# Taps of one token block moved from TensorE to VectorE in a fused sequence-mixing and feed-forward kernel

## The chip, the cores and the metric

The kernel runs on one core of one Trainium2 chip. Five engines of that core work side by side, each through its own queue in order: TensorE (PE in the profile; its weight loads are PEld), VectorE (DVE), ScalarE (ACT), GpSimd (POOL) and SyncE (SP), which here only issues transfers. The metric is the device time of one launch in microseconds, the median of several runs. Lower is better.

## The reference

All tensors are bf16. `q`, `k`, `v` are 2048 tokens by 640 channels.

```
x       = layernorm(q)
k_shift = sum over t in 0..3 of k[token - t] * shift_k[:, t]     # four taps per channel
kv      = k_shift * v
y       = causal long convolution of kv with ssm_k (2048 taps)   # by FFT
h       = q + x * (y + kv * ssm_D)
out     = h + (silu(LN(h) @ w_gate) * (LN(h) @ w_up)) @ w_down   # 640 -> 1728 -> 640
```

The part that the change touches is `k_shift * v`, for the last quarter of the tokens.

## The kernel before

**Blocks.** The 2048 tokens are cut into 4 blocks of 512. Partition p of a block holds tokens 4p to 4p+3, so a tile of a block is 128 x (4 x 640). For block i the kernel makes `kv` (the taps), takes its transform (`xf`), multiplies it with the transforms of the filter blocks (`p0i`, `p1i` and so on: product of token block j and filter block i-j, all summed into the tile Y of block i), transforms back (`iv`), adds the residual and normalises, and runs the feed-forward part (`fg` and `fu` for gate and up, `dn` for down). A feed-forward block has two halves of 256 tokens; names such as `fg2.11` mean block 2, half 1, group 1.

**Order.** Every operation is first recorded as a named task with the memory it reads and writes (`_Graph.add`). The dictionary `PLAN` then gives, for each engine, a list of task numbers: that is the order of its queue. `arrange` and `emit` only add the waits that memory, PSUM and the order require. Task numbers count the tasks in the order of recording. The string `units` gives each PSUM tile one of four units of two banks; a TensorE task that opens a tile waits until the former tile of that unit has been read.

**The taps of block 3 before.** `kvload(3)` records a transposing transfer `kT3` of 528 tokens of k (channels on partitions) into `kT` and the load `v3` of v into `kvo` (tasks 652 and 653). `taps(3)` records three groups, for channel pieces 0, 2 and 4 (tasks 654 to 662): `tp3.*` on TensorE (70 steps, each as two matmuls of 64 rows with the diagonal tap weights, L731), `ke3.*` on ScalarE (copy from PSUM to `XT`, L455) and `kv3.*` on VectorE (product with v, written over `kvo`, L742).

**What follows.** `xf3.jc` (L619) multiplies row j of `kvo`, that is the tokens 4p+j, with a cosine or sine table; its results are copied out by `xf3e.*` to `XH1` and `OS`, and `xb3.*` (L634) combine them on VectorE. The spectra then go into `p33`, `yb3.0` to `yb3.5` (L651) turn the sum into four rows, `iv3.*` (L919) transform back. For block 2 the same tasks are `yb2.*` and `iv2.*`: `iv2.0` and `iv2.1` need `yb2.4`, `iv2.2` and `iv2.3` need `yb2.5`. An `iv` is followed by `ivN.e` (ScalarE), `g` (VectorE), `m` and `s` (ScalarE statistics), `v` (VectorE), `r` (GpSimd), `n` (VectorE) and `ht` (a transposing transfer into `hnT`); the `fg` and `fu` of a half need the two `ht` of that half.

**Accumulating transfers.** `addto` (L568) issues from GpSimd a transfer that adds one SBUF tile to another. Several sums of the kernel are made so already, with 640 KB each.

**The branch of the change.** It is in the code before, but no block uses it (`DT` and `DTA` are empty):

```
load("wst", wst[...], ... [[0, P], [1, 4 * D]] ...)             # the 640 x 4 weights, to every partition
load("kh%d" % i, kh[...], ... (N * i - 3) * D, [[4 * D, P], [1, 7 * D]])   # seven tokens per partition
g.add("wbr", "act", ... out=wbr[:], in_=wst[:].rearrange("p d u -> p u d") ...)
for j0 in (1, 0):
    kin = [[-D, 4], [2 * D, 2], [1, D]] from kh[:, 3 + j0]      # 4 taps x 2 tokens x 640
    win = wbr[:].unsqueeze(2).to_broadcast([P, 4, 2, D])
    a: tm = kin * win                       # VectorE, 128 x 5120
    b: tm[:, 0:2] += tm[:, 2:4]             # transfer from GpSimd where i is in DTA, else VectorE
    c: tm[:, 0] += tm[:, 1]                 # VectorE, 128 x 1280
    d: kvo[:, j0:4:2] = tm[:, 0] * kvo[:, j0:4:2]   # VectorE, 128 x 1280
```

`kh` lies over `C2` and `wst` and `tm` lie over `XH1`, which the products `p13` read; `wbr` lies over `kT`.

Of the kernel before, what the change touches and what calls it, by code (L numbers as in the profile page):

```python
# [50 lines left out]
class _Graph:  # L51
# [128 lines left out]
    def emit(self, block):  # L180
# [74 lines left out]

PLAN = {
    "pe":
        "20 22 26 29 24 25 28 32 35 31 34 27 30 33 68 65 62 41 39 72 70 46 56 48 52 50 58 54 44 86 88 78 80 139 84 137 76 74 82 "
        "96 102 90 92 104 94 100 204 98 301 298 159 168 304 155 177 186 212 153 151 311 313 141 147 143 149 309 145 307 317 237 "
        "319 315 236 321 241 202 218 242 220 210 216 214 208 206 247 261 256 246 266 251 257 267 262 365 356 271 383 278 374 "  # L260
        "279 283 287 291 422 421 486 483 489 431 496 498 426 492 502 427 504 494 436 500 506 432 441 451 446 442 447 463 464 "
        "660 654 657 456 452 468 555 546 472 573 564 476 665 663 669 667 671 673 677 675 592 593 597 602 598 603 607 617 613 "
        "612 622 618 623 627 634 647 726 717 635 639 744 643 735 754 753 763 759 758 764 768 778 795 773 774 779 784 788 783 "
        "796 799 805 802 808 "
        "",
    "act":
        "1 18 5 37 36 40 73 71 57 49 53 51 59 55 45 89 79 87 81 140 138 77 85 75 83 97 103 91 93 105 95 101 205 99 302 299 160 "
        "169 162 305 163 171 178 172 213 187 156 152 312 154 142 148 314 150 144 146 308 189 318 310 190 239 320 316 180 322 "
        "238 181 243 203 329 219 221 211 217 215 209 207 330 331 332 333 244 334 335 258 336 249 337 338 248 339 268 252 254 "
        "253 263 259 264 340 357 366 272 384 276 359 269 360 273 274 368 280 277 375 369 377 284 386 378 288 387 424 423 487 "  # L270
        "484 490 292 433 497 499 428 503 493 429 495 505 501 507 437 434 514 515 516 438 517 443 439 518 519 448 444 461 520 "
        "521 449 522 523 453 465 524 661 655 525 658 457 454 458 459 469 556 547 558 559 549 550 574 565 576 577 567 666 670 "
        "668 568 674 678 676 594 595 685 599 600 686 604 688 689 690 605 608 691 610 609 692 693 614 615 694 619 695 620 624 "
        "625 628 630 629 727 718 729 720 730 721 745 747 736 748 738 739 756 755 761 760 766 765 770 769 771 775 776 793 781 "
        "780 786 785 791 789 790 794 "
        "",
    "dve":
        "23 21 38 69 66 67 64 63 42 43 116 108 109 47 110 112 113 111 117 114 115 118 120 119 121 60 122 61 124 123 126 127 128 "
        "130 129 132 131 134 133 135 106 136 161 196 170 107 164 306 303 300 173 166 195 175 188 199 198 157 179 324 191 200 "
        "323 201 325 240 182 326 193 327 184 328 197 222 345 344 347 346 245 348 350 349 352 351 341 250 353 255 354 260 355 "  # L280
        "395 392 358 393 265 394 270 367 398 275 361 385 400 363 403 370 376 405 372 397 399 402 404 379 407 388 408 381 409 "
        "425 488 485 491 410 390 412 411 414 413 417 416 508 509 430 510 418 511 435 512 419 513 440 531 530 533 532 445 534 "
        "450 536 535 541 526 537 538 540 539 542 543 455 544 460 528 662 462 557 545 548 656 560 473 659 551 562 575 566 553 "
        "582 477 578 664 672 679 680 569 580 681 571 682 683 596 583 584 585 587 588 589 687 601 590 701 702 606 704 703 611 "
        "706 707 709 708 616 696 697 621 632 626 711 631 633 712 714 713 699 715 716 728 719 636 731 722 733 724 640 746 737 "
        "644 740 749 700 757 648 751 742 762 767 772 777 782 787 792 797 800 806 803 809 "
        "",
    "pool":
        "19 17 15 16 125 165 174 158 192 183 223 225 224 342 396 362 281 371 285 401 380 289 406 389 343 293 420 415 527 466 "
        "470 561 474 552 478 579 570 684 586 591 529 705 710 698 637 732 723 641 645 750 649 741 "  # L290
        "",
    "sp":
        "0 2 3 8 4 6 10 7 230 9 11 13 14 235 296 226 12 229 297 227 481 231 167 176 228 234 295 233 194 185 482 232 364 282 373 "
        "290 391 294 286 382 480 653 652 471 563 554 467 475 479 581 572 651 734 725 638 752 646 743 642 650 798 807 801 804 "
        "810 "
        "",
    "units":
        "0131203132312001201201213230032110213023012230313133033220021021122013200230230222110332013110130232003210332301202110"
        "01310112312301210312031012210230131023033303012010313012013"
        "",  # L300
    "fills": {
        "wb0": ["zmem", 3],
        "k0t4.0": ["zmem", 1],
    },
}
# [2 lines left out]
def bass_sequential_preLN__ssm_conv_h3__swiglu_ffn__prompt_kernel(  # L308
# [43 lines left out]
    PAIR = True  # L352
    BN = (0,)
    BNH = ()
    DT = ()
    DTA = ()
    HALF = (0, 1, 2, 3)
    R4K = ()
    R4X = (1,2,3)
# [19 lines left out]
    with ExitStack() as es:  # L379
# [66 lines left out]
        def load(name, dst, src, kb, engs="sp", **kw):  # L446
            return g.add(name, engs, lambda e, n: e.dma_start(dst, src), ("ld", kb), w=[dst], dma=True, **kw)
# [119 lines left out]
        def addto(name, dst, src):  # L567
            return g.add(name, "pool", lambda e, n: e.dma_start(dst, src, accum_op=ALU.add, max_dma_last_dim=4096), ("acc", 2 * int(np.prod(dst.shape))),  # L568
                         r=[dst, src], w=[dst], dma=True)
# [117 lines left out]
        def kvload(i):  # L687
            if i in DT:
                load("wst", wst[:].rearrange("p d u -> p (d u)"), bass.AP(A_shift_k.tensor, A_shift_k.offset, [[0, P], [1, 4 * D]]), 655360)
                load("kh%d" % i, kh[:].rearrange("p j d -> p (j d)"), bass.AP(K2.tensor, K2.offset + (N * i - 3) * D, [[4 * D, P], [1, 7 * D]]), 1146880)  # L690
                load("v%d" % i, kvo[:], tokens(V2, i), 655360)
                return
            tload("kT%d" % i, kT[:], K2[N * i - 16:N * (i + 1), :], N + 16, D)
            load("v%d" % i, kvo[:], tokens(V2, i), 655360)

        def taps(i):
            if i in DT:
                g.add("wbr", "act", lambda e, n: e.activation(out=wbr[:], in_=wst[:].rearrange("p d u -> p u d"), func=ACTF.Copy), ("ac", 4 * D), r=[wst[:]], w=[wbr[:]])
                for j0 in (1, 0):
# [6 lines left out]
                          r=[kh[:], wbr[:]], w=[tm[:]])  # L706
                    if i in DTA:
                        addto(nm + "b", tm[:, 0:2], tm[:, 2:4])
# [517 lines left out]
```

## Time and profile before

| what | value |
|---|---|
| median of 3 runs | 260.73 us (259.1 to 261.67) |
| profiled execution | 259.3 us; its span 257.3 us |
| PE busy | 249.3 us, 97% of the span |
| DVE busy | 200.0 us, 78% |
| ACT busy | 184.5 us, 72% |
| POOL busy | 58.5 us, 23% |
| granted clock | 1.0 throughout |

The span runs from the first to the last instruction. A share of busy time is a mean over the span; which engine sets the time is read from the stage in question. The timeline lists instructions in order of start, neighbours of one kind merged; the time of an instruction is longer than the distance to the next one on the same engine, because neighbours overlap a little. For instance VectorE products of 128 x 5120 take 2.82 us each, and two that follow each other start 2.74 us apart. Sums over a queue are made from such distances.

### The profile page before, as it was taken

The page shows a single profiled execution, that of the slowest core. Times are in us where ns is not written, and L with a number is a line of the kernel's source. Part 1 is how long each engine was busy: PE and PEld are TensorE (multiplying, and loading weights), DVE is VectorE, ACT ScalarE, POOL GpSimd, SP SyncE. Part 2 cuts the span into 40 slices and gives each one's busy share as a digit, 9 for nine tenths or more (in the row PEclk, how much of TensorE's full clock was granted, in tenths as well). Part 3 has the DMA queues.
Part 4 walks back from the last instruction along what each step waited for, and adds up shares of the span by engine and source line. Part 5 has one row for each costly group of instructions (what it writes and reads, how often), then busy time and mean ns, then how long its engine had stood idle before and what let it go on. Part 6 is the DMA issues. An engine that isn't in the chain of part 4 may idle for free.

```text
span 257.3 us, 5303 instructions
## 1 busy us (share of the span) xinstructions
PE 249.3 (97%) x2253; PEld 195.1 (76%) x2253; DVE 200.0 (78%) x256; ACT 184.5 (72%) x302; POOL 58.5 (23%) x56
## 2 busy tenths in 40 slices
PE   7999997999999999979999999999999999999995
PEld 4878773587888766868888866788886678888763
DVE  3689999999999998999999988999958524211242
ACT  2489999999996894577899789749981854516410
POOL 1001003082312052860030813333230314000000
PEclk9999999999999999999999999999999999999999
DMA  6998946788994058786946035497870152700011
GB/s 220 335 328 210 402 155 133 221 205 190 329 190 87 0 82 124 128 164 153 273 87 124 3 51 117 118 221 133 148 135 3 25 104 33 149 0 3 0 42 60
DMA packets 37620, 35.29 MB, mean 137 GB/s; under 512 B 21203, under 2 KB 32478, under 8 KB 37598
## 3 DMA queue, kind: packets, MB, share of 16 engines
q1 hardware_dynamic: 31792, 23.82, 33.2%
q0 software_dynamic: 5792, 11.14, 25.1%
q8 instruction: 17, 0.28, 0.5%
q14 instruction: 5, 0.04, 0.1%
q10 hardware_dynamic: 14, 0.01, 0.0%
HBM read 16.55 MB, written 2.62 MB: 75 GB/s over the span
## 4 chain that ended last, share of the span: by engine, by line
PE 62%; DVE 20%; ACT 11%; DMA 5%; issue 1%; SPq 0%; DVEq 0%
PE ps L1029 32%; PE ps L1115 16%; DVE tt L777 6%; PE ps L599 3%; DMA Y<-tt 3%; DVE Y L777 3%; PE ps L731 2%; ACT KO L455 2%; PE ps L919 2%; ACT C L455 2%; PE ps L581 2%; DVE C L777 2%; PE ps L992 2%; PE ps L619 2%; DMA k0n<-in_A_k_dram 1%; DVE gu L1050 1%
## 5 line engine op out<-in xcount | busy, mean ns | idle before, releaser
L1115 PE MATMUL ps<-Wd,gu 128*128 128x320 bf16 (+1 forms) x420 | 58.7, 300 | 0.0
L1115 PEld LDWEIGHTS ps<-Wd,gu 128*128 128x128 bf16 (+1 forms) x420 | 38.7, 97 | 18.4 <-issue 3.6
L777 DVE TENSOR_TENSOR tt<-XH,C 128x2560 bf16<-128x2560 bf16 (+1 forms) x31 | 47.8, 1571 | 1.5 <-DMA Y<-tt 0.9
L1050 DVE TENSOR_TENSOR gu<-gu,ub 128x1024 bf16<-128x1024 bf16 (+1 forms) x32 | 19.8, 620 | 26.2 <-ACT gu L1037 13.7
L1037 ACT ACTIVATE gu<-ps 128x1024 bf16<-128x1024 f32 (+1 forms) x32 | 29.4, 923 | 12.1 <-PE ps L1029 12.0
L1029 PE MATMUL ps<-hnT,GB 128*128 128x256 bf16 x280 | 34.0, 273 | 0.9 <-ACT XT L455 0.9
L1042 ACT ACTIVATE ub<-ps 128x1024 bf16<-128x1024 f32 x24 | 24.6, 1024 | 13.3 <-PE ps L1029 11.5
L1029 PE MATMUL ps<-hnT,UB 128*128 128x256 bf16 x280 | 33.8, 273 | 0.0
L1029 PEld LDWEIGHTS ps<-hnT,GB 128*128 128x128 bf16 x280 | 27.3, 98 | 4.3 <-ACT XT L455 1.0
L1029 PEld LDWEIGHTS ps<-hnT,UB 128*128 128x128 bf16 x280 | 27.3, 98 | 3.4 <-ACT KO L455 0.2
L1029 PE MATMUL ps<-hnT,GA 128*128 128x256 bf16 x240 | 28.8, 273 | 0.0
L1029 PE MATMUL ps<-hnT,UA 128*128 128x256 bf16 x240 | 28.5, 273 | 0.1
L837 POOL TENSOR_TENSOR mv<-mv,half 128x1 f32<-128x1 f32 x16 | 21.3, 1335 | 24.7 <-DVE mv L835 24.7
L1029 PEld LDWEIGHTS ps<-hnT,UA 128*128 128x128 bf16 x240 | 23.4, 98 | 3.4 <-ACT C L455 0.5
L1029 PEld LDWEIGHTS ps<-hnT,GA 128*128 128x128 bf16 x240 | 23.4, 98 | 3.2 <-DVE XH L458 0.3
L840 ACT ACTIVATE qo<-xh 128x640 bf16<-128x640 bf16 x28 | 21.0, 749 | 5.7 <-DMA xh<-in_A_q_dram 3.2
L581 PE MATMUL ps<-KT,tab 128*128 128x320 bf16 x128 | 19.6, 300 | 1.6 <-ACT K3r L455 0.7
L934 ACT ACTIVATE qo<-ps,one,st 128x640 bf16<-128x640 f32 x16 | 13.7, 886 | 9.8 <-PE ps L919 9.0
L568 POOL DMA_DIRECT2D xh<-RB x12 | 10.7, 888 | 34.7 <-DVE RB L1132 23.2
L581 PEld LDWEIGHTS ps<-KT,tab 128*128 128x128 bf16 x128 | 11.5, 98 | 8.2 <-ACT K3r L455 1.6
L837 POOL TENSOR_TENSOR st<-st,half 128x4 f32<-128x4 f32 x4 | 7.9, 1986 | 33.6 <-DVE st L832 21.8
L455 ACT ACTIVATE XH<-ps 128x640 bf16<-128x640 f32 x19 | 13.3, 736 | 1.5 <-PE ps L619 0.7
(112 smaller groups left out, 384.8 us busy)
## 6 DMA issues: line engine op xcount, KB each, us to landing
C<-US POOLq DMA_DIRECT2D x6, 640.0 KB, 5.9
kc<-in_A_ssm_k_dram SPq DMA_DIRECT2D x4, 640.0 KB, 10.6
xh<-in_A_q_dram SPq DMA_DIRECT2D x4, 640.0 KB, 5.5
out_dram<-xh SPq DMA_DIRECT2D x15, 160.0 KB, 2.0
kvo<-in_A_v_dram SPq DMA_DIRECT2D x3, 640.0 KB, 4.4
xh<-RB POOLq DMA_DIRECT2D x12, 160.0 KB, 3.0
Wd<-in_B_w_down_dram SPq DMA_DIRECT2D x1, 1280.0 KB, 7.8
C<-K3r POOLq DMA_DIRECT2D x2, 640.0 KB, 7.9
```

Source lines behind the costliest of these rows:

```text
L455: return e.activation(out=dst[1], in_=src(), func=ACTF.Copy, scale=scale)
L568: return g.add(name, "pool", lambda e, n: e.dma_start(dst, src, accum_op=ALU.add, max_dma_last_dim=4096), ("acc", 2 * int(np.prod(dst.shap ...
L581: last = e.matmul(pt.f(c, W), tab[:, f, cs, j], src[:, j, c * W:(c + 1) * W], start=(j == js[0]), stop=(j == js[1]))
L777: g.add(nm, "dve", lambda e, n_: e.tensor_tensor(out=d, in0=a, in1=b, op=op), ("sb", n * D), r=[a, b], w=[d])
L837: g.add(name + "r", "pool", lambda e, n: e.tensor_tensor(out=dst, in0=tmp, in1=hf, op=ALU.pow), ("pp", 4), r=[tmp, half[:]], w=[dst])
L840: g.add(name + "m", "act", lambda e, n: e.activation(out=junk, in_=x, func=ACTF.Identity, scale=-1.0 / D, accum_out=sm), ("aa", D, 0), r=[ ...
L934: g.add(nm + "e", "act", lambda e, n, pt=pt, q2=q2, s=s, j=j: e.activation(out=q2, in_=pt.f2(W), func=ACTF.Identity, scale=s[:, 3, j:j + 1 ...
L1029: last = e.matmul(pt.f(q // 2, 256, o=256 * (q % 2)), w[:, c, f0:f0 + P], hnT[:, c, cols], start=(c == 0), stop=(c == NC5 - 1))
L1037: g.add("sg%d.%d%d" % (i, h, gp), "act", lambda e, n, pa=pa, gv=gv, nf=nf: e.activation(out=gv, in_=pa.f(0, 256 * nf).rearrange("p (f x) - ...
L1042: g.add("su%d.%d%d" % (i, h, gp), "act", lambda e, n, pb=pb: e.activation(out=ub[:].rearrange("p b x -> p (b x)"), in_=pb.f(0, 1024), func ...
L1050: g.add("mu%d.%d%d" % (i, h, gp), "dve", lambda e, n, gv=gv, ubv=ubv: e.tensor_tensor(out=gv, in0=gv, in1=ubv, op=ALU.mult), ("sb", 256 * ...
L1115: last = e.matmul(pt.f(c, W), gu[k, fb, col(i, j)], Wd[k, fb, c * W:(c + 1) * W], start=st, stop=sp)
```

## The change

`DT` and `DTA` become `(3,)`: block 3 takes the branch above, with sum b as an accumulating transfer. Tasks 652 to 662 (eleven) become 652 to 663 (twelve): `wst`, `kh3`, `v3`, `wbr`, `tv3.1a` to `tv3.1d` (656 to 659, for the odd tokens of each four), `tv3.0a` to `tv3.0d` (660 to 663, for the even ones). All later numbers rise by one, so `xf3.10` is 663 before and 664 after. The three PSUM tiles of `tp3` go. With it comes a whole new `PLAN`: other orders on all engines, other units, and some copies on another engine (of those near block 3: `rs1.2`, `rs1.3`, `rs2.2`, `rs2.3`, `xf3e.10`, `xf3e.00`, `la3.0x` and two `gd` go from VectorE to ScalarE, `xf3e.01` and `kf2e.000` from ScalarE to VectorE). The first filler of TensorE is put ahead of `wb4`, which now comes before `wb0`.

```
     "pe":
...
-        "660 654 657 456 452 468 555 546 472 573 564 476 665 663 669 667 671 673 677 675 592 593 597 602 598 603 607 617 613 "
...
+        "464 456 468 472 555 546 476 564 573 664 666 670 668 676 674 672 678 593 592 598 597 603 602 607 617 613 618 612 622 "
...
     "dve":
...
-        "450 536 535 541 526 537 538 540 539 542 543 455 544 460 528 662 462 557 545 548 656 560 473 659 551 562 575 566 553 "
-        "582 477 578 664 672 679 680 569 580 681 571 682 683 596 583 584 585 587 588 589 687 601 590 701 702 606 704 703 611 "
...
+        "409 425 410 485 488 491 412 411 381 414 413 430 416 417 508 509 418 510 435 511 419 512 440 513 656 530 445 531 532 "
+        "533 450 534 455 540 536 535 526 538 537 460 539 541 658 542 543 659 544 528 660 548 557 545 582 551 560 583 553 585 "
+        "562 662 584 663 566 680 681 675 575 682 683 684 587 596 569 578 588 590 580 571 589 601 702 703 704 705 606 708 707 "
...
-        "wb0": ["zmem", 3],
+        "wb4": ["zmem", 3],
...
-    DT = ()
-    DTA = ()
+    DT = (3,)
+    DTA = (3,)
```

By name, around block 3, the new queues read:

```
PE   ... dn1.0b fg1.13 dn1.1 dn1.2 iv2.1 iv2.0 dn1.3 iv2.2 iv2.3 xf3.10 .11 .31 .30 .20 .01 .00 .21 fu2.00 fg2.00 ...
DVE  ... p13.1a p13.1b xb2.0 xb2.1 p13.1c xb2.2 mu1.02 xb2.3 p13.1d xb2.4 mu1.03 xb2.5 tv3.1a p22.0a mu1.10 ...
     ... p22.1e yb2.1 tv3.1c yb2.2 yb2.3 tv3.1d yb2.4 la2w tv3.0a iv2.0g iv2.1g yb2.5 p23.0a iv2.0v iv2.1v p23.0b
     iv2.0n p23.0d iv2.1n tv3.0c p23.0c tv3.0d iv2.2g xb3.0 xb3.1 xf3e.01 ...
ACT  ... la2.0s su1.03 wbr su1.10 gd1.0 la2.0x sg1.10 ... iv2.3e iv2.2e xf3e.31 xf3e.10 la2.3x xf3e.11 xf3e.30 ...
POOL ... p13.1e tv3.1b ra1.0 la2r ra1.1 p13.0e ra1.2 tv3.0b iv2.0r ra1.3 iv2.1r ...
SP   ... x2 wst kh3 v3 out1.0 out1.1 ht2.0 ht2.1 ...
```

Before, TensorE had `dn1.1 iv2.1 iv2.0 dn1.2 iv2.3 iv2.2 dn1.3 xf3.11` in that place.

## The prediction

> **What bounds the kernel now.** I read the page's busy shares first, then busy time by stretch, then the chain that ended last, then VectorE's timeline around block 3. The shares say that TensorE is nearly full; the stretches say which other engine has room, and where.
>
> ```profile
> PE 249.3 (97%) x2253; PEld 195.1 (76%) x2253; DVE 200.0 (78%) x256; ACT 184.5 (72%) x302; POOL 58.5 (23%) x56
> ```
>
> ```profile
> core 0: us, PE busy (x) PEld busy (x) DVE busy (x) ACT busy (x) POOL busy (x), PEclk, DMA share, GB/s
> 12.90:57.00 44.10, 42.03 (x392) 30.32 (x390) 42.27 (x56) 42.89 (x70) 7.76 (x5) 1.00 0.86 237
> 57.00:114.50 57.50, 56.13 (x524) 44.71 (x522) 56.00 (x62) 46.25 (x79) 22.16 (x18) 1.00 0.71 146
> 114.50:149.70 35.20, 35.20 (x352) 29.45 (x352) 35.17 (x39) 29.65 (x49) 8.13 (x5) 1.00 0.56 124
> 149.70:166.80 17.10, 16.86 (x128) 11.73 (x128) 15.01 (x30) 15.19 (x28) 5.10 (x7) 1.00 0.46 97
> 166.80:198.40 31.60, 31.60 (x280) 26.96 (x279) 27.76 (x36) 21.18 (x35) 8.49 (x7) 1.00 0.68 131
> 198.40:254.70 56.30, 56.21 (x466) 44.04 (x463) 17.18 (x31) 25.04 (x40) 5.97 (x8) 1.00 0.21 45
> ```
>
> The third number is PE, the fifth DVE. VectorE's 78% is a mean: from 12.9 to 149.7 us it is idle for 1.83 + 1.50 + 0.03 = 3.4 us of 136.8, and all its spare time lies after 198.4, when the spectra are done. Block 3's taps sit before that, at 140 to 156 us, with both engines full.
>
> The chain that ended last, cut around block 3 (start, length, what), shows what the taps cost TensorE and where block 2's feed-forward begins:
>
> ```profile
> 135.92 3.77 PE ps L1115 x28
> 139.69 2.28 PE ps L731 x70
> 141.97 3.93 PE ps L1029 x35
> 145.90 3.88 PE ps L1115 x28
> 149.78 1.24 PE ps L919 x8
> 151.02 3.77 PE ps L1115 x28
> ...
> 160.94 1.68 PE ps L619 x10
> ```
>
> The 2.28 us of L731 are all three `tp3`. L919 at 149.78 is `iv2.1` and `iv2.0`. VectorE's timeline has what released it, `yb2.4`:
>
> ```profile
> 148.22 1.49 DVE L651 TENSOR_TENSOR Y<-OS,Y 128x2560 bf16<-128x2560 bf16 x1
> ```
>
> It ends at 149.7, just as TensorE finishes `dn1.1`. The old order meets there to 0.1 us. `xf3` ends and `fg2.00` starts at 162.6; from then to 254.6 TensorE is never idle for more than 0.1 us.
>
> **What the change removes.** On TensorE 2.28 us (`tp3`); the other matmuls are only reordered, so a change with VectorE always in time would give 259.3 - 2.3 = 257.0. On ScalarE three copies, 0.91 + 0.91 + 0.49 = 2.3 us, against which stands `wbr`: copies of 640 and 1280 elements there are 0.59 and 1.13 us apart, so 2560 elements are about 2.2 us, an estimate from these rows. Its read is strided; the block-0 copies of 1024 elements that regroup tokens take the usual 1.02 us, so I add nothing. If stride doubled it, ScalarE would lose 2.2 us where the next paragraphs find 3.8 us of cover. On VectorE three products, 0.60 + 0.60 + 0.33 = 1.5 us.
>
> **What it adds on VectorE, up to `yb2.4`.** Products and sums of 5120, 2560 and 1280 elements stand 2.74, 1.40 and 0.73 us apart in this trace:
>
> ```profile
> 45.42 2.82 DVE L777 TENSOR_TENSOR Y<-XH,C 128x5120 bf16<-128x5120 bf16 x1
> 48.16 2.82 DVE L777 TENSOR_TENSOR tt<-XH,C 128x5120 bf16<-128x5120 bf16 x1
> ```
>
> The broadcast weight operand (a middle step of 0) is in no row. From below: the rows above, 2.74, since the second has a middle step backwards too and pays nothing. From above: products that read PSUM, 512 elements 0.60 and 1024 elements 1.13 us apart, 1.035 ns per element, 5.4 us for 5120. I take 2.74, the nearest row in form: 16-bit operands in SBUF, runs of 640.
>
> The Trainium skill, page "VectorE: DVE Perf Modes", section "What auto-detection actually checks", has 16-bit operands go two per cycle where every tensor steps by one, and says nothing against a repeated middle dimension. By it the product costs 2.74; with one element per cycle it would be 5.3, an estimate from that page's clock. No row here shows a broadcast.
>
> Comparing the two VectorE orders up to `yb2.4`, the new one has more: `kf2e.000` 0.8, `tv3.1a` 2.74, `tv3.1c` and `tv3.1d` 1.46, `mu1.13` 0.33; swapped early copies cancel to 0.1. That is 5.4 us on a queue without idle time: `yb2.4` ends at 149.7 + 5.4 = 155.1. TensorE gets to `iv2.1` after `dn1.2` instead of `dn1.1`: 149.8 - 2.3 + 3.8 = 151.3. So it **waits 3.8 us there**.
>
> **Then up to `tv3.0d`.** The queue between is `la2w` 0.06, `tv3.0a` 2.74, two `g` 0.80, `yb2.5` 1.40, `p23.0a` 1.40, two `v` 0.12, `p23.0b` 1.40, `n` 0.36, `p23.0d` 0.73, `n` 0.36, `tv3.0c`, `p23.0c`, `tv3.0d` 2.19: 11.6 us, so `tv3.0d` ends at 166.7. `tv3.0b` is issued after `tv3.0a`, at 158.0; six transfers of its kind (US into C) have a median of 5.9 us to landing, so it lands at 164; `tv3.0c` comes up at 164.5. The transfer hides, by half a microsecond.
>
> TensorE meanwhile: `iv2` to 156.3, `dn1.3` to 160.1, `iv2.2` and `iv2.3` (after `yb2.5`, at 160.1) to 161.2, then four `xf3` on the odd rows. `xf3.20` needs the even rows: 166.7, a second wait of over 3 us. `xf3.11` and `xf3.30` are copied to `XH1`, where `tm` lies, so they wait for `tv3.0d` too. Two copies of 0.59 and that of `xf3.20` free its unit for `fu2.00`: 166.7 + 0.1 + 3 x 0.59 = 168.6. Normalisation gives no earlier start: `iv2.1n` ends at 164.3, `ht` takes 2.6, so `hnT` is there at 167.
>
> `fu2.00` at 168.6 instead of 162.6 is **+6.0 us**, the 2.3 saved already inside.
>
> **Afterwards.** The same matmuls, 92 us of them, follow in both. VectorE has 21.4 us from `tv3.0d` to `p33.1c`, so 189 with small waits, its transfer lands at 195, and `yb3.4` is done near 200; `dn2.0` ends at 168.6 + 29.4 + 2.7 = 200.7. `iv3` does not wait, the tail is of the old length, and nothing is given back.
>
> **Loads.** `wst` and `kh3` can only go when `p13` has read `XH1` and `C2`, after `p13.1b`, at 124.8 by the same comparison. They bring 1.8 MB. GA, itab and UB, 2.4 MB in sequence, took 10.2 us from first issue to last landing, so 8.2 us: `kh3` is there at 133.0 to 133.3, where VectorE, after 8.1 us of `xb2` and `p13` work, asks for it at 132.9. I add 0.3. `wbr` holds ScalarE from 127.5 until `wst` lands (about 130.4), with `su1.10` behind it, done at 133.6; TensorE needs that unit at 133.8, so the wait hides, and delay there only shortens the one at `iv2.1`. `v3` behind `kh3` is wanted 15 us later.
>
> **The sum.** 259.3 + 6.0 + 0.3 = 265.6 against the profiled time. The median of the runs lies 1.4 above that execution; I put half of it in: **266.3 us**.
>
> **Rivals.**
> - VectorE makes good all its 3.4 us of idle time before 149.7. `yb2.4` then ends at 151.7, every step after moves with it: +2.6 + 0.3, 262.9. For it: all queues are reordered from the start. Against: two thirds of it lies at waits for loads, copies and transfers that remain. I count it as the low end of the forecast's own range, 262.5 to 268.
> - The broadcast product runs at the PSUM rate: 2 x 2.65 more, all on the path: 271.6. For it only the lack of a row.
> - `kh3` or `tv3.0b` lands 2 us later (p02.e took 8.4 us, p13.0e 9.8, in company): 268.5. For it: both have under 0.6 us of cover.
> - The other side, faster: the VectorE work never holds TensorE, which keeps its 2.3 us: 259.3 - 2.3 + 0.7 = 257.7. It decides at `xf3.20`, where TensorE would be at 158.7: `tv3.0d` would have to end 8 us before my sum. For it speaks ScalarE's and TensorE's new order; against it that VectorE has 3.4 us to give. If it found 5 to 6 us, the result would be no change, 260 to 261.
>
> **How the numbers follow.** Forecast 0.69, slow product 0.08, late transfers 0.13, no change 0.05, faster 0.05. About 1% (2.6 us) is what a measurement of this kernel tells from no change. Slower by over 1%: 0.69 + 0.08 + 0.13 = 0.90; within 1%: 0.05; faster: 0.05. The range reaches from the idle time made good, 262.5, to the slow product, 272.
>
> **What would show it.** No L731 for block 3, and PE's busy time down by about 2.3 us; `tv3.*a` rows (L705, tm<-kh,wbr, 128x5120) of 2.82 us; a PE wait of 2 to 4 us for VectorE ahead of L919 near 151 to 155 us, and one of 3 to 5 us ahead of L619 near 162 to 167; block 2's first L1029 near 168.6; VectorE full from 13 to 167. The prediction is wrong if VectorE ends `yb2.4` before 152, if the L705 rows are near 5.4, or if PE loses time after 169.

## The result, and the profile after

The changed kernel took **274.0 us** (median of 4 runs, 270.24 to 275.18) against 260.91 us for the kernel before beside it (4 runs, 259.1 to 261.67): ratio 1.042, 95% interval 1.033 to 1.052. In two later sessions the same kernel came to 273.79 us (272.34 to 277.0) and 271.98 us (268.04 to 274.84), where the kernel before stood at 257.58 and 258.46: ratios 1.061 (1.054 to 1.067) and 1.043 (1.035 to 1.051). The medians are over all runs, while the ratios and their intervals leave out every run that is more than 1.5% slower than the fastest of its kernel. So the change costs 13 to 16 us by the medians and 11 to 16 by the ratios, where 6 were forecast, and the changed kernel spreads from 268.0 to 277.0 us over 14 runs, while most runs of the kernel before within a session lie 2 us apart at most. Both facts need an explanation.

The profiled execution took 273.32 us, its span is 271.3. The busy shares of the page:

```profile
PE 252.0 (93%) x2183; PEld 193.7 (71%) x2183; DVE 202.7 (75%) x254; ACT 188.8 (70%) x306; POOL 78.4 (29%) x57
```

PE has 70 matmuls fewer, worth 2.28 us, and is yet busy 2.7 us longer: something made matmuls slower. POOL is busy 20 us longer with the same twenty powers and two accumulating transfers more. Busy time by stretch; the stretches are cut where TensorE ends `dn1.1` (149.4) and the first matmuls of block 2's feed-forward, `fu2.00` (179.2):

```profile
core 0: us, PE busy (x) PEld busy (x) DVE busy (x) ACT busy (x) POOL busy (x), PEclk, DMA share, GB/s
114.50:149.40 34.90, 34.07 (x287) 26.98 (x284) 33.54 (x37) 29.57 (x47) 9.71 (x5) 1.00 0.63 162
149.40:179.20 29.80, 19.85 (x110) 11.99 (x111) 24.88 (x32) 15.59 (x29) 17.15 (x9) 0.83 0.68 132
179.20:212.00 32.80, 32.80 (x293) 28.10 (x291) 26.28 (x37) 26.60 (x44) 8.92 (x7) 1.00 0.52 99
212.00:268.70 56.70, 56.62 (x469) 44.55 (x467) 13.44 (x29) 24.57 (x39) 5.78 (x8) 1.00 0.19 42
```

The loss is in the second row. Between the same two points the kernel before needs 15.1 us (149.8 to 164.9, the end of `fg2.00`, its first one); here it is 29.8, with TensorE idle for 10 us and its granted clock at 0.83. After that nothing is lost in this execution: 89.4 us to the last matmul, 89.7 before. TensorE's timeline in that stretch (start, length, what; in brackets the wait and what ended it):

```profile
150.70 3.95 PE L1115 MATMUL ps<-Wd,gu 128*128 128x320 bf16 x28 [1.33 <-ACT gu L1091]
156.74 1.26 PE L919 MATMUL ps<-Y,itab 128*128 128x320 bf16 x8 [2.09 <-DVE Y L651]
157.93 5.59 PE L1115 MATMUL ps<-Wd,gu 64*128 64x320 bf16 x28
165.21 1.26 PE L919 MATMUL ps<-Y,itab 128*128 128x320 bf16 x8 [1.70 <-DVE Y L651]
...
172.95 2.32 PE L619 MATMUL ps<-kvo,tab 128*128 128x320 bf16 x8 [3.67 <-DVE kvo L714]
175.06 4.09 PE L1029 MATMUL ps<-hnT,UA 128*128 128x256 bf16 x20
178.98 2.35 PE L1029 MATMUL ps<-hnT,GA 128*128 128x256 bf16 x20
```

Two things are to be read here. The waits that the prediction named are there: for `yb2.4` (156.74) and for `tv3.0d` (172.95). With them come waits that it did not have: 1.33 us ahead of `dn1.2` (150.70), for a ScalarE copy that had itself waited for VectorE, and 1.70 us for `yb2.5` (165.21). And the same work takes longer behind some of them: `dn1.3` 5.59 us where `dn1.2`, of the same 28 matmuls, takes 3.95; `fu2.00` 4.09 where `fg2.00` takes 2.35; the last eight `xf3` 2.32 where later runs give 1.25. Together that is 1.64 + 1.74 + 1.07 = 4.45 us, and the granted clock is why:

```profile
158.00:160.00 2.00, 2.00 (x9) 1.06 (x10) 2.00 (x1) 0.00 (x0) 1.71 (x2) 0.53 0.54 82
160.00:162.00 2.00, 2.00 (x11) 1.21 (x10) 0.51 (x1) 1.52 (x3) 0.42 (x1) 0.61 0.97 173
...
174.00:176.00 2.00, 2.00 (x10) 1.30 (x9) 1.97 (x4) 1.10 (x3) 0.00 (x0) 0.50 1.01 186
176.00:178.00 2.00, 2.00 (x11) 1.43 (x10) 1.36 (x3) 2.00 (x6) 0.00 (x0) 0.50 1.07 142
```

The third number from the end is the clock: 0.53 to 0.61 under `dn1.3`, 0.50 under `fu2.00`. In the kernel before it is 1.0 throughout. The chain that ended last, cut to that stretch, shows a second thing that was not expected:

```profile
148.54 9.02 POOL st L837
157.56 2.90 DMA xh<-RB
160.46 0.02 issue
160.48 0.02 ACT RB L1131
160.50 0.67 issue
161.18 1.66 ACT qo L934 x2
162.84 0.02 issue
162.86 0.89 DVE xh L941 x2
```

L837 at 148.54 is `la2r`, a power of 128 x 4 numbers on GpSimd. Two of the other three of its kind in this execution took 1.04 and 1.54 us; the third, `la1r` near 78, took 9.28. Behind it in GpSimd's queue stands the transfer `ra1.1`, for that `rs1.2` on ScalarE waits, behind that `iv2.1e` and `iv2.0e`, and for these VectorE at `iv2.0g`. VectorE's rows show both ends of it, and the one late load:

```profile
134.44 2.82 DVE L705 TENSOR_TENSOR tm<-kh,wbr 128x5120 bf16<-128x5120 bf16 x1 [0.90 <-DMA kh<-in_A_k_dram]
...
157.62 0.17 DVE L865 TENSOR_SCALAR st<-st 128x4 f32<-128x4 f32 x1 [0.94 <-POOL st L837]
162.86 0.89 DVE L941 TENSOR_TENSOR xh<-xh,qo 128x640 bf16<-128x640 bf16 x2 [2.35 <-ACT qo L934]
```

The broadcast product takes 2.82 us, the plain rate.

### The profile page after: what moved, and what is told of

It reads as the page before. It is cut to its first block, busy times and chain, and to the rows that moved or that the text cites. A ratio compares the mean times of both kernels' runs of the same rounds, so it can differ in the third digit from the quotient of the medians.

```text
span 271.3 us, 5172 instructions
## 1 busy us (share of the span) xinstructions
PE 252.0 (93%) x2183; PEld 193.7 (71%) x2183; DVE 202.7 (75%) x254; ACT 188.8 (70%) x306; POOL 78.4 (29%) x57
## 4 chain that ended last, share of the span: by engine, by line
PE 41%; DVE 32%; POOL 12%; DMA 10%; ACT 2%; issue 1%; SPq 1%; DVEq 0%; ACTq 0%
PE ps L1029 22%; DVE tt L777 11%; PE ps L1115 10%; POOL st L837 7%; DVE Y L777 5%; POOL mv L837 4%; PE ps L599 3%; DMA kh<-in_A_k_dram 3%; DMA kc<-in_A_ssm_k_dram 3%; DMA Y<-tt 3%; PE ps L581 2%; DVE gu L1050 2%; DVE XH L634 2%; DVE C L561 2%; PE ps L992 2%; DVE xh L941 1%
## 5 line engine op out<-in xcount | busy, mean ns | idle before, releaser
L1115 PE MATMUL ps<-Wd,gu 128*128 128x320 bf16 (+1 forms) x420 | 59.9, 305 | 1.3 <-ACT gu L1091 1.3
L837 POOL TENSOR_TENSOR mv<-mv,half 128x1 f32<-128x1 f32 x16 | 25.2, 1579 | 38.8 <-DVE mv L835 38.7
L1042 ACT ACTIVATE ub<-ps 128x1024 bf16<-128x1024 f32 x24 | 24.6, 1023 | 15.2 <-PE ps L1029 12.5
L1029 PE MATMUL ps<-hnT,UA 128*128 128x256 bf16 x240 | 30.4, 283 | 0.5 <-ACT XT L455 0.3
L837 POOL TENSOR_TENSOR st<-st,half 128x4 f32<-128x4 f32 x4 | 20.9, 5225 | 23.9 <-DVE st L832 21.2
L1029 PEld LDWEIGHTS ps<-hnT,UA 128*128 128x128 bf16 x240 | 24.3, 102 | 4.7 <-ACT XH L455 0.5
L1029 PEld LDWEIGHTS ps<-hnT,GA 128*128 128x128 bf16 x240 | 23.2, 98 | 4.7 <-DMA hnT<-qo 1.2
L568 POOL DMA_DIRECT2D xh<-RB x12 | 11.3, 939 | 38.3 <-ACT RB L1131 23.4
L619 PE MATMUL ps<-kvo,tab 128*128 128x320 bf16 x48 | 10.3, 330 | 5.9 <-DVE kvo L714 3.7
```

Source lines behind the costliest of these rows:

```text
L619: last = e.matmul(pt.f(c, W), tab[:, 0, cs, j], src[:, j, c * W:(c + 1) * W], start=True, stop=True)
L837: g.add(name + "r", "pool", lambda e, n: e.tensor_tensor(out=dst, in0=tmp, in1=hf, op=ALU.pow), ("pp", 4), r=[tmp, half[:]], w=[dst])
L1029: last = e.matmul(pt.f(q // 2, 256, o=256 * (q % 2)), w[:, c, f0:f0 + P], hnT[:, c, cols], start=(c == 0), stop=(c == NC5 - 1))
L1042: g.add("su%d.%d%d" % (i, h, gp), "act", lambda e, n, pb=pb: e.activation(out=ub[:].rearrange("p b x -> p (b x)"), in_=pb.f(0, 1024), func ...
L1115: last = e.matmul(pt.f(c, W), gu[k, fb, col(i, j)], Wd[k, fb, c * W:(c + 1) * W], start=st, stop=sp)
```

## The experiments

Times are medians; each is to be read against the kernel before in the same session (a "call" in the expectations). The sessions were not all on one chip, and the start of an execution varies by a microsecond, so traces are compared from a point of their own: from the end of `kv2.4` (VectorE, near 116) to the end of block 2's first `fu` or `fg`. That stretch is 50.5 us before, and 62.4 in the profiled execution of the changed kernel.

### First session: the power, and the clock (kernel before: 258.34 us)

`e1_la2w_early` lets VectorE stand still while the power runs; `e2_ra_first` takes the transfer out from behind it.

```diff
 VectorE (e1):  ... p22.1a la2v
+               la2w
                p22.1d p22.1c ... tv3.1d yb2.4
-               la2w
                tv3.0a ...
```

```diff
 GpSimd (e2):   ... tv3.1b ra1.0
-               la2r
                ra1.1
+               la2r
                p13.0e ra1.2 ...
```

> The changed kernel with one move in VectorE's queue: la2w (128x4, needs the GpSimd power la2r) right behind la2v, so that VectorE stands still until la2r is done. Theory A (VectorE's unbroken run of two-input products keeps la2r from finishing, 9.0 us, and la2r holds ra1.1, rs1.2, iv2.1e and so tv3.0d): la2r takes 1 to 2 us, VectorE loses about 1.5 us there, rs1.2 starts near 156 in place of 160.5, VectorE's waits before la2w (0.9) and before iv2.0g (2.35) go; time about 271 (269.5 to 272.5) against 274.0. Rival (la2r is slow for a reason of its own, whatever VectorE does): la2r stays near 9 us, VectorE stands still that long, time 279 or more.

> The changed kernel with one move in GpSimd's queue: the transfer ra1.1 ahead of the power la2r instead of behind it. Theory A: la2r stays at 6 to 9 us, but ra1.1 is issued near 151.6 in place of 157.6, rs1.2 runs near 155.5 in place of 160.5, iv2.1e follows la2w at once near 158, the 2.35 us wait of VectorE before iv2.0g goes; time about 271 (270 to 272.5). Rival (ra1.1 was not what held the rest; VectorE's added work alone makes the delay): within 1 us of the changed kernel, 273 to 275.

Measured: **e1 272.64 us** (270.82 to 274.42; ratio 1.055), **e2 270.8 us** (270.44 to 274.37; 1.048). GpSimd's timeline of e1:

```profile
149.22 1.04 POOL L833 TENSOR_TENSOR st<-st,half 128x4 f32<-128x4 f32 x1
```

The power takes 1.04 us when VectorE stands still; in e2 it took 5.26 us, and again ended only in a gap of 0.9 us on VectorE. So VectorE's instructions can hold it. The stretch falls from 62.4 to 58.2 us in both, by the size of the theory; but the median hardly moves. The reason came with the next session: in the second profile of the unchanged kernel the power took 1.50 us by itself, and the stretch 57.9. The hold is one of the things that differ from run to run; e1 and e2 remove what only some runs have.

`e3_fill` puts dummy matmuls of 512 columns, whose results nobody reads, into TensorE's waits; `f1_fill_again` is the same kernel in the third session.

```diff
     "fills": {"wb4": ["zmem", 3], "k0t4.0": ["zmem", 1],
+              "dn1.2": ["tab0", 6], "iv2.1": ["tab0", 8], "iv2.2": ["tab0", 7], "xf3.20": ["tab0", 15],
     },
```

> The changed kernel with dummy matmuls on the cosine table in TensorE's waits: 6 before dn1.2, 8 before iv2.1, 7 before iv2.2, 15 before xf3.20; nothing else moves. If the granted clock of 0.5 to 0.6 between 158 and 162 and between 172 and 178 us comes from TensorE standing still and costs time: clock 1.0 throughout, fu2.00 takes 2.2 us in place of 3.9, dn1.3 3.8 in place of 5.5, time about 272 (271 to 273). Rival (the slow clock falls into time that TensorE would wait anyway): 273.5 to 275, the dummy matmuls only fill waits.

> The run e3_fill again, as the standard for this call: 266.5 to 270, clock 1.0, ratio to the kernel before 1.03 to 1.04.

Measured: **e3 268.24 us** (266.57 to 270.29; ratio 1.038), **f1 267.79** (267.13 to 271.44; 1.040), granted clock 1.0 in both, stretch 56.2 and 56.5, against 57.9 in the second profile of the changed kernel: more work on TensorE, and less time in this stretch. For the whole time it is not yet a proof, since the changed kernel was not in these sessions and its first ratio, 1.042, lies within e3's interval (1.031 to 1.045); f2 against f3 and the last session compare side by side.

`e5_old_taps` keeps the new order of the program and puts the old taps of block 3 back.

```diff
-    DT = (3,)
-    DTA = (3,)
+    DT = ()
+    DTA = ()
 TensorE:  ... dn1.0b
+          tp3.4 tp3.0 tp3.2
           fg1.13 dn1.1 ...
 ScalarE:  ... su1.12
+          ke3.2 ke3.0 ke3.4
           la2.2s ...
 VectorE:  ... yb2.4 la2w
-          tv3.0a
+          kv3.4 kv3.0 kv3.2
```

> The changed kernel's order with the old taps put back (kT3, tp3, ke3, kv3 in place of wst, kh3, wbr and tv3; the taps' three matmul groups before fg1.13, the products after la2w). VectorE has 7.4 us less, TensorE 2.3 us more than in the changed kernel. Theory (the taps on VectorE cost the time): 262 to 265, most of the 13 us come back, though la2r may still hold ra1.1. Rival (the new order of the whole kernel costs it, whichever engine makes the taps): 269 or more.

Measured: **270.88 us** (269.11 to 273.04; ratio 1.048). The theory missed by 6 us and the rival has the number, but the run is spoiled by the place that I gave to `ke3`: ScalarE waited 2.6 us for TensorE there, its `la2.3s` came late, and VectorE stood 5.2 us at `la2v`. It is repeated below as `g2_old_taps`.

### Second session: order or taps (kernel before: 257.58 us)

> The changed kernel as it is, as the standard for this call. 270 to 275 us, +11 to +14 over the kernel before of the same call; a wait of over 3 us ahead of L619 and a granted clock near 0.5 behind it in the profile.

The changed kernel again: **273.79 us** (272.34 to 277.0). Its profile has the wait of 3.67 us at L619 and a clock of 0.88 to 0.91 in the stretches behind it; and the power is quick, so that TensorE ends `fu2.00` 3.4 us earlier than in the first profile (175.8). But it loses that again, and more, later:

```profile
191.20 2.31 PE L1029 MATMUL ps<-hnT,GA 128*128 128x256 bf16 x10 [2.84 <-DMA hnT<-qo]
```

TensorE waits 2.84 us for the second half of `hnT`, and the ten matmuls behind it take 2.31 us instead of 1.25. From the chain of the same execution, the transposing transfer `ht2.2`:

```profile
183.98 0.02 DVE gu L1050
184.00 7.15 DMA hnT<-qo
191.15 0.05 issue
```

It takes 7.15 us; in the first profile 2.88, in the kernel before 2.57. At 184.28 GpSimd sends the accumulating transfer `p23.1e`, and `xb3.4` landed only at 184.25, with `ht2.3` still under way. The same is in e2 (6.59 us), `e6_eighth` (7.66) and `e7_sums_dve` (6.33), where TensorE waits 2.3 to 3.3 us.

`e4_old_order` is the counterpart of e5: the old order of every queue, with the new taps put in by hand.

```diff
 VectorE:  ... mu1.03
+          tv3.1a
           p22.0b ... p22.1e
+          tv3.1c
           yb2.2 yb2.3 mu1.12
+          tv3.1d
           yb2.4 mu1.13 la2w
+          tv3.0a
           gd1.1 ... iv2.0n
+          tv3.0c tv3.0d
           p23.0a ...
 GpSimd:   ... p13.1e
+          tv3.1b
           p13.0e la2r ra1.0 ra1.1
+          tv3.0b
           iv2.1r ...
```

> The order of the kernel before on every engine, with the new taps put in by hand where the old ones stood: tv3.1a behind mu1.03, 1c and 1d ahead of yb2.2 and yb2.4, tv3.0a behind la2w, 0c and 0d behind iv2.0n; everything is computed. Theory A (the taps' work on VectorE, in a queue that has no room, holds TensorE whatever the order): up to yb2.4 4.2 us more on VectorE, so yb2.4 ends near 154, and 6.9 us more up to tv3.0d, against 2.3 that TensorE saves: +4.5 to +7, 263 to 266, and up to 269 if the clock falls behind the waits. Rival B (the new order of the whole program costs the time, not the taps): within 1.5 us of the kernel before or faster, 256 to 260.

Measured: **269.94 us** (268.71 to 270.77; ratio 1.046). The rival that puts all the cost on the new order falls: the old order with the new taps, placed by hand, is 12 us above the kernel before. Two of TensorE's rows:

```profile
144.99 0.97 PE L1026 MATMUL ps<-hnT,GB 128*128 128x256 bf16 x5 [4.39 <-ACT RB L1128]
159.36 5.41 PE L1112 MATMUL ps<-Wd,gu 128*128 128x320 bf16 x28 [3.17 <-DVE gu L1089]
```

The product delays the `mu` of the feed-forward on VectorE, these delay ScalarE's copies, and TensorE waits for its PSUM units; `la2r` took 9.71 us here too, and 28 matmuls behind the wait took 5.41 us.

`e6_eighth` cuts the taps' VectorE work in the new order; sums b, c and d are cut in the same way, and the taps of the other 560 channels are left out.

```diff
-tensor_tensor(out=tm[:], in0=kin, in1=win, op=ALU.mult)
+tensor_tensor(out=tm[:, :, :, 0:80], in0=kin[:, :, :, 0:80], in1=win[:, :, :, 0:80], op=ALU.mult)
```

> The changed kernel in its own order, with tv3.*a, b, c and d cut to 80 of the 640 channels; the taps of block 3 for the other 560 channels are left out. VectorE has 2 x (2.5 + 0.6 + 0.6) = 7.4 us less to do, TensorE and ScalarE the same. Theory A: la2v still waits for la2.3s on ScalarE near 148, so the first 2.5 us are lost; yb2.4 ends near 155.3 instead of 156.7, tv3.0d 5 us earlier, and the end comes 4 to 7 us earlier than in the changed kernel: 265 to 269 where that takes 272. Rival B (the new order costs the time): 271 to 274, as without the cut.

Measured: **268.0 us** (265.78 to 269.15; ratio 1.039), 5.8 below the changed kernel: theory A's number. But the trace gives the taps only part of it. The stretch from `kv2.4` is 55.5 us against 57.9, so 2.4 us come from there; `kv2.4` itself ends at 114.7 instead of 117.9, before a single tap of block 3 ran. Of these 3.2 us 0.6 are a later start (the first GpSimd power, `la0r`, starts at 22.87 and at 23.42); 2.6 are won on the way, where another power, `la1r` at 78, took 2.20 us instead of 9.28. VectorE's wait for ScalarE behind it, in the first profile of the changed kernel and in e6:

```profile
88.65 0.49 DVE L941 TENSOR_TENSOR xh<-xh,qo 128x640 bf16<-128x640 bf16 x1 [1.91 <-ACT qo L934]
```

```profile
87.31 0.49 DVE L941 TENSOR_TENSOR xh<-xh,qo 128x640 bf16<-128x640 bf16 x1 [0.30 <-ACT qo L934]
```

And 268 is still 10 us above the kernel before with hardly any taps on VectorE. TensorE still waits, and the same matmuls are still slow behind the wait:

```profile
165.31 2.31 PE L619 MATMUL ps<-kvo,tab 128*128 128x320 bf16 x8 [2.50 <-DVE kvo L714]
```

`e7_sums_dve` makes the two sums `tv3.*b` on VectorE.

```diff
-    DTA = (3,)
+    DTA = ()
 VectorE:  ... yb2.1
+          tv3.1b
           tv3.1c ... iv2.1n
+          tv3.0b
           tv3.0c ...
```

> The changed kernel with the two sums tv3.*b made by VectorE (1.40 us each, ahead of tv3.*c) in place of the accumulating transfers; everything is computed. Theory A (VectorE's queue is the bound, the transfers are hidden): +1.4 to +2.8 us over the changed kernel, 273 to 277. Rival C (the transfer is what tv3.0c waits for, or it holds up other transfers): the same or faster, 268 to 272.

Measured: **276.93 us** (271.76 to 277.64), 3.1 above the changed kernel of the same session, a little more than theory A's 1.4 to 2.8; but the ranges overlap (the lowest run of e7 is 271.76 us, that of the changed kernel 272.34), so the times alone do not show it. The traces do: two sums of 1.40 us cost 2.8 on VectorE, the wait for `yb2.4` grows from 2.09 to 3.61 us, and the stretch from 57.9 to 62.0. The accumulating transfers are the better choice there, and hidden: in the first profile `tv3.0b` lands at 169.0 and is asked for at 170.6.

### Third session: what is left (kernel before: 258.56 us)

`f2_ht_early` is e2 with the normalisations ahead of `p23.1b`, so that the transposing transfers go before `p23.1e`; `f3_ht_fill` adds the dummy matmuls; `f4_eighth_fill` has both and the cut of e6.

```diff
 VectorE:  ... iv2.2v iv2.3v
+          iv2.3n iv2.2n
           p23.1b p23.1d
-          iv2.3n iv2.2n
           p23.1c ...
```

> The changed kernel with ra1.1 ahead of la2r on GpSimd (as in e2_ra_first) and with iv2.3n and iv2.2n ahead of p23.1b on VectorE, so that SP sends the transposing transfers ht2.3 and ht2.2 a microsecond or more before GpSimd sends p23.1e; everything is computed. Theory D (in r_after, e2_ra_first and e6_eighth ht2.2 met p23.1e, took 6.6 to 7.7 us instead of 2.9 and cost TensorE 2.3 to 3.3 us of waiting and about 1 us of slow clock behind it): ht2.2 takes 2.6 to 3 us, no wait near 188, and 3 to 4.5 us less than those runs: 266.5 to 269.5. Rival (the late wait is VectorE's lateness, the transfers are not the cause): ht2.2 still takes over 5 us or the wait moves, 270 to 273.

> f2_ht_early and the dummy matmuls of e3_fill in TensorE's waits (6, 8, 7 and 15, ahead of dn1.2, iv2.1, iv2.2 and xf3.20). Theory B (the slow clock behind the waits costs 3 to 5 us of its own): clock 1.0 and 264 to 267, below f1_fill_again by 0 to 3 and below f2_ht_early by 2.5 to 4. Rival (the clock's slow stretches are in time that TensorE has anyway): as f2_ht_early.

> e6_eighth (tv3.* on 80 of 640 channels, the taps of the other 560 left out) with the two moves of f2_ht_early and dummy matmuls in the waits (4, 4 and 9, ahead of dn1.2, iv2.1 and xf3.20). It prices the new order alone, without most of the taps' VectorE work, without the collision and without the slow clock. If the new order costs nothing by itself: 255 to 258, TensorE's 2.3 us saved. If what is left are the waits that e6_eighth shows ahead of dn1.2, iv2.1 and xf3.20 and between the xf3 (5.7 us, less 2.3): 259 to 262. If the collision and the clock were not additive: 264 or more.

Measured: **f2 271.29 us** (270.31 to 271.7; ratio 1.050), **f3 268.84** (267.2 to 270.0; 1.039), **f4 266.15** (263.5 to 267.71; 1.026). In f2 the wait near 188 is gone (`ht2.2` takes 4.0 us, all ten GA matmuls 1.25), and from `fu2.00` to the last matmul it is 89.5 us, where r_after needs 94.0 and e2 93.6. The collision and its price are shown in the traces, but the median is 0.5 above e2's, not 3 below: like the held power, it does not come in every profile, and in which of the other runs it came is not known. f3 against f2 gives 2.5 us for the clock, and here the runs of the two do not overlap (267.2 to 270.0 against 270.31 to 271.7). f4 misses its 259 to 262: the new order, nearly without the taps' VectorE work and the slow clock, and without the collision, is still 7.6 us above the kernel before, 4.9 in its fastest run. It is not the new order alone, though: the loads, `wbr`, the transfers and the two gates at `yb2.4` and `tv3.0d` are still in it.

### Fourth session: three repairs (kernel before: 258.8 us)

`g1_la1_still` is e3 with one more VectorE instruction, behind `la1v`, that waits for `la1r`.

```diff
-            if i > 1:
-                g.add("la%dw" % i, ... scalar1=-1.0, ...
+            if i:
+                g.add("la%dw" % i, ... scalar1=-1.0 if i > 1 else 1.0, ...
```

> e3_fill with one tiny VectorE instruction more, right behind la1v, that reads the result of GpSimd's power la1r (times 1.0), so that VectorE stands still while the power runs; everything is computed. Theory E (VectorE's instructions hold the power, and la1r's 9.28 us cost the chain 1.5 to 2.5 us by way of ra0.0): la1r takes 1.0 to 1.2 us, VectorE loses 1.1 us there and wins 1.6 at the next iv1.1g, TensorE's wait near 105 falls from 1.0-1.4 to under 0.5, dn1.1 ends 1 to 2 us earlier than in e3_fill (150.5) and f1_fill_again (149.0), and the time is 265 to 267. Rival (the power's length is hidden): 267 to 270, dn1.1 as before or 1 us later.

Measured: **266.84 us** (265.96 to 268.17; ratio 1.029). GpSimd's rows of f1 and of g1:

```profile
78.04 9.28 POOL L833 TENSOR_TENSOR st<-st,half 128x4 f32<-128x4 f32 x1 [3.36 <-DVE st L831]
```

```profile
79.09 1.03 POOL L833 TENSOR_TENSOR st<-st,half 128x4 f32<-128x4 f32 x1 [3.32 <-DVE st L831]
```

That VectorE holds the power is shown a second time. That it costs the time is not: TensorE's wait near 105 is 1.51 us (1.22 in f1), and from the start of `la0r` near 23 us to the end of `kv2.4` both need 94.1 us. What the quick power gives, the standing still (1.16 us on VectorE) and later waits take.

`g2_old_taps` is e5 with `ke3` behind `la2.2s`, in the order in which TensorE delivers, and `la2v` behind `yb2.1`; `g4_old_order` is e4 with three moves that free ScalarE's and GpSimd's queues.

```diff
 ScalarE (g2):  ... la2.2s
+               ke3.4 ke3.0 ke3.2
 VectorE (g4):  ... mu1.11
+               tv3.1a
 GpSimd (g4):   ... p13.0e
+               tv3.1b
                ra1.0 ra1.1
+               la2r tv3.0b
```

> The new order of the whole program with the old taps of block 3: tp3 on TensorE ahead of fg1.13, their copies behind la2.2s on ScalarE in TensorE's order, the products kv3 behind la2w on VectorE, and la2v behind yb2.1 so that VectorE does not stand waiting for ScalarE; everything is computed. Theory A (the taps' VectorE work is the main cost): 2.3 us more on TensorE and 9 less on VectorE than the changed kernel; dn1.1 near 150, TensorE never waits for yb2.4, one of 1 to 3 us at the xf3: 260 to 264, within 5 us of the kernel before. Rival B (the new order is what costs): 266 to 271, as e5_old_taps (270.9).

> The order of the kernel before with the new taps, as e4_old_order, with three moves: tv3.1a behind mu1.11 instead of mu1.03, so that ScalarE's and TensorE's units come free first; tv3.1b behind p13.0e and la2r behind ra1.1 on GpSimd, so that neither holds up ra1.0, ra1.1 or p13.0e; wbr behind sv1.03. Everything is computed. Theory A (5.4 to 7 us more of VectorE's work on the way to tv3.0d, 2.3 less on TensorE, nothing else): yb2.4 near 154, and 262.5 to 266. If GpSimd's power and the clock belong to any order with that much VectorE work: 267 to 270, as e4_old_order (269.9).

Measured: **g2 272.06 us** (270.48 to 273.01; ratio 1.050), **g4 271.9** (271.13 to 275.12; 1.052). Both miss theory A. In g2 VectorE has 7 us less to do and waits for ScalarE instead, whose tap copies (2.5 us, and 1.6 us of waiting for TensorE) now stand in the way; and the first matmuls of block 2 are slow:

```profile
173.85 4.43 PE L1025 MATMUL ps<-hnT,UA 128*128 128x256 bf16 x20 [0.79 <-ACT OS L451]
```

```profile
153.69 0.42 DVE L1046 TENSOR_TENSOR gu<-gu,ub 128x512 bf16<-128x512 bf16 x1 [3.89 <-ACT ub L1042]
```

In g4 `yb2.4` ends at 154.9, as the theory said, but TensorE waits 3.29 us for a PSUM unit before that, and 3.66 us behind it for `gd1.1`, which stands behind `tv3.0a` on VectorE.

### Fifth session: the clock by itself (kernel before: 258.46 us)

```diff
 h2_fill_all:   "dn1.2": 6, "iv2.1": 8, "iv2.2": 7, "xf3.20": 15   (as e3)
 h3_fill_last:  "xf3.20": 15 alone
```

> The changed kernel, as the standard for this call: 271 to 275 us, granted clock 0.97 to 0.99.

> The changed kernel with dummy matmuls in all four waits (6, 8, 7 and 15 of 512 columns, ahead of dn1.2, iv2.1, iv2.2 and xf3.20), as e3_fill. Theory B (the clock falls behind each wait and slows the matmuls behind it): clock 1.0, dn1.3 3.95 us instead of 5.6, fu2.00 2.4 instead of 4.1, and 4 to 6 us below h1_after. Rival (that slow stretch is time TensorE has): within 1.5 us of h1_after.

> The changed kernel with dummy matmuls in the last wait alone (15, ahead of xf3.20). Theory B: the last xf3 1.25 us and fu2.00 2.4 us, dn1.3 still slow in the executions where it is slow now; 2 to 3.5 us below h1_after and 1 to 3 above h2_fill_all. Rival: as h1_after.

Measured: **h1 271.98 us** (268.04 to 274.84; ratio 1.043), **h2 268.67** (267.76 to 270.46; 1.040), **h3 267.81** (263.49 to 268.78; 1.026). By the medians the fillers win 3.3 us in h2, a little under what was expected, and 4.2 in h3, a little over. By the ratios h2 (interval 1.035 to 1.045) is not told apart from h1 (1.035 to 1.051), and h3 (1.018 to 1.034) is, but only two of its runs enter the ratio. The fastest runs of h1 and h2 are alike (268.04 and 267.76), so what the fillers take away is the upper part of the spread. In TensorE's rows of h1 and of h3, the last eight `xf3` and `fu2.00`:

```profile
168.46 2.32 PE L619 MATMUL ps<-kvo,tab 128*128 128x320 bf16 x8 [3.67 <-DVE kvo L714]
170.56 2.81 PE L1029 MATMUL ps<-hnT,UA 128*128 128x256 bf16 x20
```

```profile
169.90 1.26 PE L615 MATMUL ps<-kvo,tab 128*128 128x320 bf16 x8
171.15 2.36 PE L1025 MATMUL ps<-hnT,UA 128*128 128x256 bf16 x20
```

h3 was expected 1 to 3 us above h2 and is not: the filler ahead of `xf3.20` does all that the four do, since in these profiles `dn1.3` is fast (3.95 us) behind the wait of 2.09. h1's profiled execution took 268.04 us, the least of the 14; it has the power quick (1.49 us), `ht2.2` at little cost (0.33 us of waiting) and only 1.5 us of slow clock. It is the changed kernel nearly undisturbed, with one hold left: `la1r` took 9.28 us in it too.

No version came near the kernel before; the best median, f4's, leaves most of the taps out, and of the complete ones g1's is the lowest, 8 us above.

## Why the prediction was wrong

Three profiled executions of the changed kernel against the prediction, in us against the kernel before:

| | predicted | first | r_after | h1 |
|---|---|---|---|---|
| end of `dn1.1`, before 149.8 | -2.3 | -0.4 | +1.2 | -0.8 |
| of it: start of `la0r`, before 23.2 | 0 | -0.6 | +0.2 | -1.0 |
| of it: from there to the end of `kv2.4`, before 91.2 | 0 | +3.0 | +3.2 | +3.0 |
| of it: from there to the end of `dn1.1`, before 35.4 | -2.3 | -2.8 | -2.3 | -2.8 |
| waits from there to `fu2.00` (less 0.2 before) | +8.3 | +9.8 | +7.9 | +7.5 |
| slow clock in that stretch | 0 | +4.4 | +1.5 | +1.5 |
| from the end of `fu2.00` to the last matmul, before 89.7 | 0 | -0.2 | +4.3 | +0.3 |
| end of the last matmul (with 0.2 to 0.5 between the rows) | +6.3 | +14.0 | +15.2 | +8.7 |

The first row is the task's end less 149.8, the waits are the sum of those in brackets, the slow clock is the difference of equal groups of matmuls.

**The mechanism of the waits was right.** VectorE's queue sets both gates, at `yb2.4` and at `tv3.0d`, and h1's chain goes through the very tasks of the sum: `yb2.4`, `la2w`, `tv3.0a`, the two `g`, `yb2.5`, ..., `tv3.0d`, `xf3`. The waits, the core of the sum, were 8.3 us and came out at 7.5 to 9.8, though not in the parts forecast: ahead of `iv2.1` 2.09 us instead of 3.8, because TensorE came there at 153.6 to 156.0 instead of 151.3 and `yb2.4` ended at 155.6 to 158.1 instead of 155.1, and ahead of `dn1.2` 0.7 to 1.3 us that the sum did not have. `tv3.*a` takes 2.82 us, so the slow product was rightly held unlikely; `tv3.0b` hides. `wbr` took 2.59 us (estimated 2.2). `kh3` landed at 134.35 instead of 133.0 to 133.3 and cost 0.9 us instead of 0.3. The estimate for it rests on a misread size: GA, itab and UB are 960, 512 and 1120 KB, 2.65 MB and not 2.4, and 10.2 us scaled by size alone give 6.9 us, not 8.2. From the first issue (125.4) to the landing it was 8.9.

**The failed steps**, in the prediction's words:

- "The sum", 259.3 + 6.0 + 0.3: it has no term for TensorE's clock. The prediction named two waits of over 3 us in a stage where TensorE had never waited longer than 0.24 us, and priced the waits alone. Behind them matmuls ran at half clock: 4.4 us in the first profile, 1.5 in the two others, 2.5 us of the median between f2 and f3, 3.3 to 4.2 in the fifth session. In the first profile this is the largest term that was missing. The Trainium skill, "TensorE: Matmul & The Clock Gate", Part 1 (The HAM clock gate), describes a clock that is either half or full and is judged over windows of about 3.4 us that run free of the kernel. The trace is in keeping with the free windows, since the wait of 2.09 us is followed by a slow `dn1.3` in one profile and by a fast one in two. The page's section "HAM oscillation" warns of gaps over about 3.4 us. Here 2.09 us (first profile) and 2.5 us (e6) were enough, with shorter waits close before them.
- "Then up to `tv3.0d`": 11.6 us from `yb2.4`, counted as a queue without a wait. It took 16.2 us in the first profile and 12.7 in r_after and h1. In the first, `la2w` waited 0.94 us for the power and `iv2.0g` 2.35 us for ScalarE, behind `ra1.1`, which stood behind the power; in all, `iv2.0n` and `iv2.1n` waited 0.46 us each for GpSimd. The prediction named what is queued behind the loads on SP and behind `wbr` on ScalarE, and not what is queued behind GpSimd's `la2r`, whose length in the profile before (L837, mean 1986 ns, one of the four 4.42 us) already said that it was not a fixed cost.
- "The other matmuls are only reordered, so a change with VectorE always in time would give 259.3 - 2.3 = 257.0": not so. From `la0r` near 23 us to the end of `kv2.4` near 116 the changed kernel needs 94.2, 94.5 and 94.2 us in its three profiles, where the kernel before needs 91.2. That is 3 us gone before the first load of block 3's new taps is issued (125.4), so the taps cannot be their cause. From `kv2.4` to `dn1.1` the 2.3 us saved are there in full. In the three profiles of the new order with a short `la1r` (e5, e6 and f4) the first distance is 91.7 to 91.8, and VectorE waits 0.30 us at most at L941 near 87 instead of 1.91: most of the 3 us goes with the held power, but g1, which made it short, did not win them. Later the new order has ScalarE's `la2.3s` 6 us later (148.1 against 142.0) and more small waits, and g2, the new order with the old taps, stays 13.3 us above the kernel before. It is not a neutral carrier, and the taps are not the whole price.
- "Afterwards ... nothing is given back": right in the first profile and in h1, wrong in r_after, where `ht2.2` met two accumulating transfers and cost 2.84 us of waiting and 1.06 of slow clock behind it (the ten GA matmuls; the next ten lost 0.56 more). The prediction counted TensorE and VectorE there, not the transposing transfers, which the new order moved from a place ahead of `xb3.4` (164.6 and 165.9 before) to one beside `p23.1e`.

The rivals: no idle time was made good, the product is not slow, late transfers turned up mostly at another place (`ht2.2`, not `tv3.0b`, and `kh3` by 0.6 us). Their price in the prediction, 268.5, is a little too high: 266.3 and the 2 us give 268.3. The nearly undisturbed execution, 268.04, is within the range, but not by the sum alone: it has 3.0 us before `kv2.4` and 1.5 us of slow clock that the sum did not have, and 0.8 us less of waiting. What happens in most others is not in it.

**What stays open.** The runs that were not profiled can't be sorted by their causes. The granted clock alone does not do it: in h1 runs of 268.19 and 274.84 us have means of 0.980 and 0.981. That the held power, the collision and the slow clock each come and go is shown; how often, is not. Of the 13 us, 3 are lost before block 3's taps and belong to the new order. How much more it would cost with a fair place for the old taps is not settled: e5 and g2 were ordered by hand, as were e4 and g4, and each of the four met a full ScalarE or a full GpSimd queue of its own.

## What to carry to other kernels

Where a change puts a wait of two microseconds or more on a TensorE that never waited, add to the wait the matmuls behind it at half clock; a few dummy matmuls in the wait took 2.5 us off the median here (f3 against f2) and 3 to 4 in the last session. On a core whose VectorE has no idle time, allow for a GpSimd power that ends only at VectorE's next standstill, and look at what is queued behind it. And when the engines' orders all change, do not carry the old order's freedom from waits over to the new one: read each gate anew, with its transfers, and measure what is lost before the moved work begins.

## What the runs showed of the hardware

**A GpSimd power can be held for 9 us.** The same 128 x 4 power took 1.03 and 1.04 us while VectorE stood still (g1, e1), 1.4 to 2.2 us in some places beside VectorE, 5.26 in e2, and 9.04, 9.28 and 9.71 us in others, over seven to eleven VectorE instructions, and then ended 0.9 us after VectorE had stopped. Which it is depends on little: `la1r` took 9.28 us in thirteen profiles of the new order and 2.20 in three, with the same VectorE instructions around it. The Trainium skill, "SBUF — State Buffer", section "Who interferes with whom", has a VectorE instruction with two SBUF inputs contend with a GpSimd instruction that reads SBUF, and calls the ports that they share an exclusive lock. The traces agree that the one holds up the other; that section does not say that a hold can outlast one VectorE instruction, which lasts 0.4 to 2.8 us here, and go on over the next ones.

**A transposing transfer can be slow beside two accumulating ones.** `ht2.2` takes 2.6 us in the kernel before, and 6.3 to 7.7 us in four profiles where it is sent together with a 640 KB accumulating transfer while another is landing (4.64 us in h1, where they met too); sent the same 0.28 us ahead of `p23.1e`, but with `xb3.4` already landed, it takes 2.88 (first profile) or 2.86 us (f1).
